# Values loaded once: norms taken from the blocks' own tiles, five staging buffers, a new order

## The chip, the core and the metric

The kernel runs on one core of a Trainium2 chip. A core has TensorE (PE, matmuls), VectorE (DVE), ScalarE (ACT) and GpSimd (POOL), each with an instruction queue of its own that is worked off in order, and SyncE (SP), whose queue issues all the transfers of this kernel. 16 DMA engines move the bytes. The metric is the device time of one execution in microseconds, as the median of several runs.

## The reference

Three stages follow each other: windowed attention with a distance bias, and two feed-forward networks.

```python
# q, k, v: (4, 8, 576, 64)
scores = scale * (q @ k.T)                       # per batch and head, scale = 1/8
mask = (rel >= 0) & (rel < 128)                  # rel = query position - key position
attn = softmax(where(mask, scores + bias, -1e9))
x = (attn @ v) -> (2304, 512)                    # heads side by side

h = x @ w_in                                     # 512 -> 1024
solu = h * softmax(h)
ln = (solu - mean) / sqrt(var + 1e-6) * g_ln
x = ln @ w_out                                   # 1024 -> 512

h = x @ w2_in                                    # 512 -> 2048
out = (h * sigmoid(h)) @ w2_out                  # 2048 -> 512, (2304, 512) float32
```

## The kernel before

The 2304 tokens are 18 blocks of 128 rows; a batch is 4.5 blocks, so that blocks 4 and 13 belong to two batches each. Two blocks make a chunk of 256 tokens for the second network.

Every matmul operand is split into a high and a low float16 part, and three products (high by high, high by low, low by high) stand for one float32 product. For the split a matrix is scaled by a power of two, and that scale comes from a bound on its norm. So each weight has this life. `load_weight` brings it in pieces of 128 x 512 values of 8 bytes (512 KB each) into a staging tile `stage`; `decode` makes float32 of a piece (ACT L456, DVE L458 and L460) in the tile `W`; `gram` (PE L396) multiplies the piece by itself into an accumulator `gram` in PSUM, of which there are two in turn; `trace` or `column_max` (DVE L407, L401) take the bound from it, `norm_scale` the scale; then `split_weight` makes the two parts (L347 to L355, L533). There are 8 pieces of w_in, 8 of w_out, 16 of w2_in and 16 of w2_out, in this order. The staging tiles come from two pools: `early`, and `early2`, which serves some pieces of the first 32 slots only and gives its place to the tiles `g` of the second network later.

The values v go the same way twice. `v_norm(b)` loads batch b in five pieces into tiles `t` (L601) and takes their norm, on PE by `gram` for batches 0 and 1, on ACT by squares (L607) for 2 and 3; `V_AT` says with which block it is ranked. `v_load(i)` loads block i again into a tile `vraw` (L627), of which there are three, and `v_split(i)` makes the two parts `vs` (L347 or L348, and L635).

A block then runs: scores on PE (L681), bias and maximum on DVE (L707), exp on ACT (L712), the softmax's two halves `a` (L342, L343, L354, L355), their transposes by DMA (L739, `aT`), the product with the values (L766), its scaling on DVE (L779), the transpose `xT`, w_in (L813), the layer norm (L827 to L863), its halves and transposes `lnT`. A chunk runs w_out (L913) into `y` (L918, L921), w2_in (L950) with its gate (L959 to L963) and w2_out (L977). A block is joint (`JOINT` is J) if two head pairs' scores share the score tile and L766 writes into `mm1`, the one PSUM buffer that L813 and the layer norm use as well.

No order is written out by hand. `Sched` collects all operations with their dependencies and a rank, which `at` works out from three tables (`RANK`, `SLOPE`, `LATER`), and lists them for each engine in a fixed order before the kernel runs. Strings such as `PICK`, `E_W` and `NORM` say which engine takes an operation that several could. Since each queue is worked off in order, an operation that waits holds everything behind it on its engine; and SP, which issues all loads and transposes, waits in the same manner for a buffer to come free.

```python
more = slot0 < 32 and (at + z) % 3 == 2
st = Buf(early2 if more else early, [P, 512, 2], U32, "stage", N_MORE if more else N_STAGE)
```

Of the kernel before, what the change touches and what calls it, by code (L numbers as in the profile page):

```python
# [17 lines left out]
P = 128  # L18
# [280 lines left out]
def fused_kernel(ctx, tc, qk, qn, kn, vt, rel, w_in, w_out, g_ln, w2_in, w2_out, out):  # L299
# [99 lines left out]
    def column_max(c, acc, f):  # L399
        junk = Buf(early, [P, 4, P], BF16, "junk4", 1)  # L400
        v(552, lambda: V.tensor_tensor_reduce(junk.tile, c.tile.rearrange("p (a b) -> p a b", a=4),  # L401
                                              unit.tile.unsqueeze(1).to_broadcast([P, 4, P]), 1.0, 0.0, ALU.mult, ALU.max,
                                              acc[:, f:f + 1]), [c, unit], [junk, (acc, f)])

    def trace(c, acc):
        junk = Buf(early, [P, P], BF16, "junk", 1)
        v(P + 40, lambda: V.tensor_tensor_reduce(junk.tile, c[:, 0:P], unit.tile, 1.0, 0.0, ALU.mult, ALU.add, acc.tile),  # L407
          [c, unit], [junk, acc])
# [64 lines left out]
    def load_weight(name, w, slot0, n, cols, gain=None, columns=False):  # L473
# [114 lines left out]
    def v_norm(b):  # L588
        s.at("vnorm", V_AT[b])
        on_pe = V_NORM[b] == "P"  # L590
        acc = Buf(const, [P, 1 if on_pe else 5], F32, f"vacc{b}")
        flat = vt[b * S:(b + 1) * S, :].rearrange("a (e f) -> (a e) f", f=256)
        flat = flat.rearrange("(p r) f -> p (r f)", p=P)
        c = Buf(ps_early, [P, 512], F32, "gram", 2) if on_pe else None
        for j, (a, n) in enumerate(((0, 512), (512, 512), (1024, 512), (1536, 512), (2048, 256))):
            def go(j=j, a=a, n=n):
                st = Buf(const, [P, 512], F32, "t", N_T)

                def src():
# [24 lines left out]
    def v_load(i):  # L624
        s.at("vload", i)
# [393 lines left out]
    def block(i):  # L1019
# [6 lines left out]
        v_load(i)  # L1026
# [15 lines left out]
    for c in range(NB // 2 + 1):  # L1042
# [7 lines left out]
        while n < until:  # L1050
# [12 lines left out]
RANK = {"aturn": 8423.8, "av": 1271.8, "evac": -1036.7, "exp": 5647.5, "gate": -1017.5, "in": -427.9, "in2": 228.9,  # L1063
        "load": -3059.8, "lparts": -74.7, "max": -199.5, "max1": 533.1, "norm": -6342.9, "out": -1828.4,
        "out2": 6637.3, "parts": -1334.6, "qk": 3187.5, "s0": 424.5, "s16": 305.7, "s32": 487.6, "s8": 3951.4,
        "share": -1197.1, "store": 1239.0, "table": -3844.1, "tav": -1446.6, "tevac": -831.8, "texp": -470.1,
        "tpar": 2081.3, "tscore": -124.6, "tsub": 2069.8, "vload": 134.1, "vnorm": -2996.0, "vsplit": 736.3,
        "w0": 4797.4, "w16": 195.0, "w32": 887.5, "w8": -8.4, "xturn": -457.7, "y": -155.2}
SLOPE = {"aturn": 52.72, "av": -35.24, "evac": 8.76, "exp": 31.4, "gate": -17.8, "in": 25.51, "in2": -9.86,
         "load": 45.12, "lparts": 17.82, "max": -37.75, "max1": 22.31, "norm": -12.53, "out": 11.91, "out2": 31.11,  # L1070
         "parts": 0.14, "qk": 15.72, "s0": -0.41, "s16": 2.12, "s32": -6.31, "s8": 33.71, "share": 8.67,
         "store": -32.52, "table": 14.94, "tav": 5.28, "tevac": -13.95, "texp": 21.39, "tpar": 19.28, "tscore": 13.35,
         "tsub": -0.49, "vload": 11.22, "vnorm": 13.38, "vsplit": 45.75, "w0": -23.31, "w16": 3.84, "w32": 2.47,
         "w8": 5.05, "xturn": 53.68, "y": -13.59}
# [154 lines left out]
```

## Time and profile before

| | us |
|---|---|
| median of three runs (738.52 to 741.9) | 738.8 |
| the profiled execution | 741.13 |
| its span, from the first to the last instruction | 739.4 |
| PE busy in the span | 681.5 (92%) |
| DVE busy | 446.9 (60%) |
| ACT busy | 350.0 (47%) |
| POOL busy | 134.3 (18%) |

The three runs lie within 0.5% of each other. Busy times are shares of one whole execution, in which the first 150 us look quite different from the rest: weights are brought in, decoded and split there, while the first blocks of attention run between. How much each engine is busy has to be read stage by stage. The granted clock is 1.00 where PE runs at its higher level of 2.4 GHz, and 0.50 at 1.2 GHz; a number between is a mean over the stage.

### The profile page before, as it was taken

The numbers are of one execution on the slowest core, as the hardware profiler recorded it, in microseconds if no ns is written. First come the engines' busy times: TensorE is split into PE (matmuls) and PEld (weight loads), VectorE is DVE, ScalarE is ACT, GpSimd is POOL, SyncE is SP. The second block draws the span as 40 slices with busy tenths as digits, with TensorE's granted clock in tenths as the row PEclk, the third lists the DMA queues.
The fourth block names the chain that finished last, engine by engine and source line by source line (L and its number), as shares of the span: only waits on it lengthen the run. The fifth ranks groups of instructions, "written<-read, shape, count | busy, mean of one in ns | idle before, by whom it ended". The sixth has DMA issues, their size and how long they took to land.

```text
span 739.4 us, 14042 instructions
## 1 busy us (share of the span) xinstructions
PE 681.5 (92%) x5541; PEld 467.1 (63%) x5541; DVE 446.9 (60%) x1141; ACT 350.0 (47%) x742; POOL 134.3 (18%) x131
## 2 busy tenths in 40 slices
PE   3556678899999999999999999999999999999997
PEld 2423347578766586667757765677567666777853
DVE  4689989899799665223655558827556663322230
ACT  5486658685564554244344446517444442232231
POOL 0053215522232401000023102302110210100000
PEclk9997589899999999999999999999999999999999
DMA  9999885357734435041435354527323430200000
GB/s 324 341 296 284 230 258 101 72 146 198 144 58 102 129 70 89 1 146 40 87 79 95 57 116 115 129 43 130 57 59 58 72 74 0 58 16 15 1 29 28
DMA packets 144034, 80.29 MB, mean 109 GB/s; under 512 B 125920, under 2 KB 126560, under 8 KB 143968
## 3 DMA queue, kind: packets, MB, share of 16 engines
q1 hardware_dynamic: 143968, 79.39, 44.5%
q8 instruction: 43, 0.70, 0.4%
q14 instruction: 23, 0.19, 0.1%
HBM read 44.24 MB, written 4.72 MB: 66 GB/s over the span
## 4 chain that ended last, share of the span: by engine, by line
PE 83%; DVE 6%; DMA 5%; ACT 2%; issue 2%; POOL 1%; SPq 1%; DVEq 0%; POOLq 0%; ACTq 0%
PE mm L977 25%; PE mm L950 24%; PE mm L913 13%; PE mm L813 13%; PE sa L681 5%; DMA aT<-a 2%; DMA stage<-in_moe_w_in_dram 2%; PE mm L766 1%; DVE W L460 1%; PE sa L766 1%; DVE e L707 1%; DVE stage L458 1%; DMA t<-in_vt_dram 1%; DMA xT<-x 1%; PE gram L396 1%
## 5 line engine op out<-in xcount | busy, mean ns | idle before, releaser
L950 PE MATMUL mm<-y,W 128*128 128x256 f16 x1728 | 208.0, 273 | 0.1
L977 PE MATMUL mm<-W,g 128*128 128x512 f16 x864 | 204.0, 379 | 0.0
L950 PEld LDWEIGHTS <-W 128*128 128x128 f16 x1728 | 166.2, 98 | 36.3 <-issue 1.0
L977 PEld LDWEIGHTS <-g 128*128 128x128 f16 x864 | 82.2, 98 | 80.0 <-issue 0.5
L913 PE MATMUL mm<-lnT,W 128*128 128x256 f16 x864 | 106.9, 275 | 2.6 <-ACT lnT L568 1.5
L813 PE MATMUL mm<-W,xT 128*128 128x512 f16 x432 | 105.7, 396 | 2.6 <-DMA xT<-x 1.0
L913 PEld LDWEIGHTS <-W 128*128 128x128 f16 x864 | 84.3, 99 | 21.2 <-issue 1.8
L712 ACT ACTIVATE e<-e,mx 128x256 f32<-128x256 f32 (+1 forms) x144 | 70.0, 487 | 52.1 <-DVE mx L707 51.9
L963 DVE SCALAR_TENSOR_TENSOR g<-t,g 128x512 f16<-128x512 f32 x72 | 57.3, 798 | 54.2 <-ACT g L962 53.7
L962 ACT ACTIVATE g<-t 128x512 f16<-128x512 f32 x72 | 45.1, 627 | 91.9 <-PE mm L977 82.6
L355 POOL TENSOR_TENSOR a<-e,a 128x512 f16<-128x512 f32 (+1 forms) x37 | 47.9, 1296 | 183.6 <-DVE a L343 132.5
L960 DVE SCALAR_TENSOR_TENSOR t<-t,mm 128x512 f32<-128x512 f32 x72 | 48.5, 683 | 49.4 <-ACT t L959 49.4
L813 PEld LDWEIGHTS <-xT 128*128 128x128 f16 x432 | 43.3, 102 | 53.5 <-issue 10.5
L959 ACT ACTIVATE t<-mm,cs 128x512 f32<-128x512 f32 x72 | 48.1, 681 | 59.6 <-PE mm L950 59.3
L681 PE MATMUL sa<-k,q 64*128 64x128 f32 x544 | 52.6, 323 | 15.1 <-DVE mx L707 8.1
L707 DVE CUSTOM_DVE_ANT_0 e<-sa,table 128x256 f32<-128x256 f32 (+1 forms) x144 | 53.7, 402 | 18.3 <-PE sa L681 9.4
L681 PEld LDWEIGHTS sa<-k,q 64*128 64x128 f32 x544 | 40.5, 210 | 28.7 <-issue 14.0
L827 DVE TENSOR_REDUCE lnst<-mm 128x1 f32<-128x1024 f32 x18 | 21.9, 1216 | 40.4 <-PE mm L813 40.4
L766 PEld LDWEIGHTS <-aT 128*128 128x128 f16 x816 | 33.1, 101 | 16.1 <-issue 7.9
L921 DVE SCALAR_TENSOR_TENSOR y<-mm,cs,y 128x512 f16<-128x512 f32 x18 | 13.2, 747 | 44.6 <-ACT y L918 44.4
L829 ACT ACTIVATE e<-mm,lnst,sig 128x1024 f32<-128x1024 f32 x18 | 21.6, 1200 | 38.4 <-DVE lnst L828 34.3
L918 ACT ACTIVATE y<-mm,cs 128x512 f16<-128x512 f32 x18 | 12.2, 686 | 55.2 <-PE mm L913 46.6
(149 smaller groups left out, 694.9 us busy)
## 6 DMA issues: line engine op xcount, KB each, us to landing
stage<-in_moe_w_in_dram SPq DMA_DIRECT2D x24, 512.0 KB, 6.6
stage<-in_moe_w_out_dram SPq DMA_DIRECT2D x24, 512.0 KB, 5.3
k<-in_kn_dram SPq DMA_DIRECT2D x18, 256.0 KB, 2.9
q<-in_qn_dram SPq DMA_DIRECT2D x18, 256.0 KB, 3.2
vraw<-in_vt_dram SPq DMA_DIRECT2D x18, 256.0 KB, 3.9
out_dram<-t SPq DMA_DIRECT2D x18, 256.0 KB, 2.0
t<-in_vt_dram SPq DMA_DIRECT2D x16, 256.0 KB, 4.5
aT<-a SPq DMA_TRANSPOSE x72, 3.3
```

Of the source, the lines that this page charges most:

```text
L355: ("G", cg(n), lambda: G.tensor_tensor(dst(), a(), b(), op), True)], r, w, pick=pick)
L681: T.matmul(SA[:, j, off + sl * P:off + (sl + 1) * P], q[rows, p, :], k[rows, p, :], start=True, stop=sl not in blank)
L707: v(n + 20, lambda j=j: V.tensor_tensor_reduce(e[:, j, lo:lo + n], SA[:, j, off + lo:off + lo + n], table[:, 2 * p + j, o:o + n], -0.125, ...
L712: act(n, lambda j=j: A.activation(e[:, j, lo:lo + n], e[:, j, lo:lo + n], AF.Exp, bias=mx[:, j:j + 1], scale=-1.0, accum_out=rs[:, 2 * p + ...
L766: T.matmul(heads(i)[:, h // 4, h % 4, :], t[:, (2 * ha + j) * nh + c, :], vb[sl][:, h, hv, :], start=(n == 0), stop=(n == 3 * nh - 1))
L813: T.matmul(pt[:, half * 512:(half + 1) * 512], x[:, hx, k, :], W16(2 * k + half, hw), start=(k == 0 and hx + hw == 0), stop=(k == KD - 1 a ...
L913: T.matmul(pt[:, ct % 2], W16(8 + k, hw)[:, ct * P:(ct + 1) * P], l[:, hx * KF1 + k, :], start=(k == 0 and hw + hx == 0), stop=(k == KF1 - ...
L950: T.matmul(pt[:, mm], W16(16 + 4 * k + m // 4, hw)[:, (m % 4) * P:(m % 4 + 1) * P], y[:, hx, k, :], start=(k == 0 and hw + hx == 0), stop= ...
L959: act(512, lambda: A.activation(t.tile, flat(pt.tile), AF.Tanh, scale=cs[:, 0:1]), [pt, (cs, 0)], [t], extra=1)
L960: v(512, lambda: V.scalar_tensor_tensor(out=t.tile, in0=t.tile, scalar=1.0, in1=flat(pt.tile), op0=ALU.add, op1=ALU.mult), [t, pt], [t])
L963: v(512, lambda: V.scalar_tensor_tensor(out=flat(g[:, 1]), in0=t.tile, scalar=2.0 ** -16, in1=flat(g[:, 0]), op0=ALU.mult, op1=ALU.subtrac ...
L977: T.matmul(pt.tile, g[:, hg, mm, b * P:(b + 1) * P], W16(32 + m, hw), start=(m == 0 and hg + hw == 0), stop=(m == KF2 - 1 and hg == 1))
```

## The change

`v_norm(b)` no longer loads anything of its own. It calls `v_load` for the blocks of its batch, and takes the norm from their tiles `vraw`, in PE by four gram matmuls per block (only a block's own 64 rows where it is shared), or on ACT by a square of 512 columns per block. The tiles stay until `v_split` has read them, so there are six `vraw` tiles (`N_VRAW`) in place of three. `v_load` returns at once for a block that is there already. The scratch tiles `junk` and `junk4` go; their writers use `sq`. Staging has three buffers and two (`N_STAGE`, `N_MORE`) in place of four and two; two of five pieces go to `early2`, in place of one of three. `V_AT` ranks the norms of batches 1, 2 and 3 with blocks 1, 9 and 10, in place of 0, 7 and 6. The three tables of ranks are new throughout, and so are some entries of the strings that pick engines; blocks 7 and 12 become joint.

```diff
     def column_max(c, acc, f):
-        junk = Buf(early, [P, 4, P], BF16, "junk4", 1)
+        junk = Buf(early, [P, 512], BF16, "sq", 2)
...
-                more = slot0 < 32 and (at + z) % 3 == 2
+                more = slot0 < 32 and (at + z) % 5 in (1, 3)
...
     def v_norm(b):
+        first, stop = b * S, (b + 1) * S
+        here = range(first // P, (stop + P - 1) // P)
+        for i in here:
+            v_load(i)
         s.at("vnorm", V_AT[b])
...
-        flat = vt[b * S:(b + 1) * S, :].rearrange("a (e f) -> (a e) f", f=256)
-        flat = flat.rearrange("(p r) f -> p (r f)", p=P)
-        c = Buf(ps_early, [P, 512], F32, "gram", 2) if on_pe else None
-        for j, (a, n) in enumerate(((0, 512), (512, 512), (1024, 512), (1536, 512), (2048, 256))):
-            def go(j=j, a=a, n=n):
-                st = Buf(const, [P, 512], F32, "t", N_T)
...
-                load(n // 2, lambda: SP.dma_start(src(), flat[:, a:a + n]), [], [st])
+        if on_pe:
+            c = Buf(ps_early, [P, 512], F32, "gram", 2)
+        else:
+            s.op([("G", 150, lambda: G.memset(acc.tile, 0.0), False)], [], [acc])
+        for n, i in enumerate(here):
+            rows = slice(max(0, first - i * P), min(P, stop - i * P))
+
+            def go(n=n, i=i, rows=rows):
+                r = vraw[i]
                 if on_pe:
                     def high(x):
...
-                    gram(c, n // P, high, [st], a // P, 17)
+                        w = r.tile.rearrange("p h d -> p (h d)").bitcast(BF16).rearrange("p (c h) -> p c h", h=2)
+                        return w[rows, x * P:(x + 1) * P, 1]
+                    gram(c, 4, high, [r], 4 * n, 4 * len(here) - 1)
                     return
-                act(n, lambda: A.activation(src(), src(), AF.Square, accum_out=acc[:, j:j + 1]),
-                    [st], [st, (acc, j)], extra=1)
+                junk = Buf(early, [P, 512], BF16, "sq", 2)
+                act(512, lambda: A.activation(junk[rows], r.tile.rearrange("p h d -> p (h d)")[rows], AF.Square,
+                                              accum_out=acc[rows, n:n + 1]), [r], [junk, (acc, n)], extra=1)
...
     def v_load(i):
+        if i in vraw:
+            return
...
-        v_load(i)
         v_split(i)
...
-RANK = {"aturn": 8423.8, "av": 1271.8, "evac": -1036.7, "exp": 5647.5, "gate": -1017.5, "in": -427.9, "in2": 228.9,
+RANK = {"aturn": 8190.5, "av": 1566.9, "evac": -3109.3, "exp": 5884.2, "gate": -1711.8, "in": -283.0, "in2": 763.1,
...
-E_W = "GGGVGGVGGVVGVVGGVGGVVGGVGVGGGGGVVVVGGGGVGGVGGGGG"
+E_W = "GGGGGGVGGVVGVVGGVGGVVGGVGVGGGGGVGVVGGGGVGVVGGGGG"
...
-JOINT = "........JJJJSJJJJJ"
+JOINT = ".......JJJJJJJJJJJ"
...
-N_STAGE = 4
+N_STAGE = 3
...
-N_VRAW = 3
+N_VRAW = 6
...
-V_AT = [0, 0, 7, 6]
+V_AT = [0, 1, 9, 10]
```

The lines of the changed kernel carry numbers some seven higher than those of the kernel before: L634 is the load of `vraw`, L642 its split, L746 the transpose `aT`.

In SP's queue at the program's start, behind the first q and k, there stands in the kernel before (`t` and `vraw` are values, `stage` a piece of a weight, `aT` a transpose of a softmax):

```order
L601 DMA t<-in_vt_dram 128x512 x4
L601 DMA t<-in_vt_dram 128x256
L601 DMA t<-in_vt_dram 128x512
L1002 DMA gcol<-in_moe_g_ln_dram 128x8x1
L627 DMA vraw<-in_vt_dram 128x512 x3
L486 DMA stage<-in_moe_w_in_dram 128x1024 x3
L601 DMA t<-in_vt_dram 128x512
L486 DMA stage<-in_moe_w_in_dram 128x1024
L601 DMA t<-in_vt_dram 128x512
L486 DMA stage<-in_moe_w_in_dram 128x1024
L601 DMA t<-in_vt_dram 128x512
L486 DMA stage<-in_moe_w_in_dram 128x1024
```

It goes on with the last `t`, two transposes and a q between, two `vraw` and the seventh and eighth `stage`. In the changed kernel the same place reads:

```order
L1009 DMA gcol<-in_moe_g_ln_dram 128x8x1
L634 DMA vraw<-in_vt_dram 128x512 x6
L486 DMA stage<-in_moe_w_in_dram 128x1024 x5
L746 DMA_TRANSPOSE aT<-a_137 128x4x128
L746 DMA_TRANSPOSE aT<-a_138 128x4x128
L652 DMA q<-in_qn_dram 128x512
L486 DMA stage<-in_moe_w_in_dram 128x1024
L634 DMA vraw<-in_vt_dram 128x512 x2
L486 DMA stage<-in_moe_w_in_dram 128x1024 x2
```

The ten `t` are gone, eight `vraw` stand where there were five, and the transposes stand ahead of the sixth piece in place of behind it.

In DVE's queue the trace of batch 1's values (`vacc_150`) stands, in the kernel before, between the first two rows of w_out's decoding and the scale of w_in:

```order
L458 TENSOR_SCALAR stage<-stage 128x512
L433 TENSOR_SCALAR nrmb<-mm 128x1
L434 TENSOR_SCALAR nrmc<-nrmb 128x1
L460 SCALAR_TENSOR_TENSOR W<-stage 128x512
L407 ISA junk,vacc_150<-gram,unit 128x128
L407 ISA vacc_150 128x1
L436 TENSOR_SCALAR nrmd<-nrmc 128x1
L438 TENSOR_SCALAR Qwin<-nrmc 128x1
```

In the changed kernel it (`vacc_123`) stands behind the layer norm of block 1, between the two rows (L458, L460) that decode the last piece of w2_in:

```order
L841 SCALAR_TENSOR_TENSOR e_857,lnst<-e_857,lnst,mm_810 128x1024
L458 TENSOR_SCALAR stage<-stage 128x512
L844 TENSOR_SCALAR lnst<-lnst 128x1
L407 ISA sq,vacc_123<-gram,unit 128x128
L407 ISA vacc_123 128x1
L460 SCALAR_TENSOR_TENSOR W<-stage 128x512
L430 TENSOR_REDUCE nrmt<-vacc_123 128x1
```

It moved behind 20 more pieces of weights. Its last tile, block 8's, is issued in the changed kernel's SP queue here, behind the transposes of block 0's layer norm and the last two pieces of w2_in (moe2_w_in, which the rows name like w_in):

```order
L746 DMA_TRANSPOSE aT<-a_794 128x8x128
L888 DMA_TRANSPOSE lnT<-ln_124 128x8x128
L486 DMA stage<-in_moe_w_in_dram 128x1024
L888 DMA_TRANSPOSE lnT<-ln_124 128x8x128
L486 DMA stage<-in_moe_w_in_dram 128x1024
L634 DMA vraw<-in_vt_dram 128x512
L486 DMA stage<-in_moe_w_out_dram 128x1024
```

In the kernel before, all of batch 1 was loaded among the first six pieces.

## Rows read from the trace of the kernel before

**Rows 1.** The page: PE's and the other engines' busy time, share, instructions.

```profile
PE 681.5 (92%) x5541; PEld 467.1 (63%) x5541; DVE 446.9 (60%) x1141; ACT 350.0 (47%) x742; POOL 134.3 (18%) x131
```

**Rows 2.** Table by stage: length, busy us (and instructions) by engine, clock, DMA share, GB/s.

```profile
0.00:18.00 18.00, 7.07 (x47) 5.07 (x47) 8.28 (x39) 10.35 (x28) 1.69 (x12) 1.00 0.92 322
18.00:37.00 19.00, 10.66 (x84) 7.50 (x83) 13.37 (x44) 8.17 (x18) 0.67 (x1) 1.00 1.13 341
37.00:92.00 55.00, 32.85 (x234) 19.06 (x232) 50.23 (x132) 40.88 (x87) 21.91 (x17) 0.78 1.00 270
92.00:143.50 51.50, 42.48 (x355) 28.90 (x354) 46.87 (x116) 36.35 (x73) 20.90 (x20) 0.83 0.58 146
143.50:208.00 64.50, 63.21 (x667) 50.80 (x665) 57.16 (x140) 39.23 (x80) 18.35 (x18) 1.00 0.64 150
208.00:700.00 492.00, 489.65 (x3974) 336.64 (x3971) 263.50 (x662) 205.45 (x443) 70.81 (x65) 1.00 0.34 71
700.00:740.00 40.00, 35.62 (x198) 19.09 (x195) 7.51 (x11) 9.57 (x15) 0.00 (x0) 1.00 0.07 27
```

**Rows 3.** Pieces of the chain that ended last: start us, us, what.

```profile
136.67 6.98 PE mm L813 x24
143.65 1.31 PE mm L950 x12
144.96 0.70 PE sa L766 x24
...
161.63 5.18 PE mm L813 x24
...
243.51 1.09 PE sa L681 x16
```

**Rows 4.** SP's timeline at the start: start us, us of issuing, what.

```profile
8.95 1.48 SPq L486 DMA_DIRECT2D stage<-in_moe_w_in_dram  x3
...
20.91 1.00 SPq L627 DMA_DIRECT2D vraw<-in_vt_dram  x2
22.18 1.60 SPq L486 DMA_DIRECT2D stage<-in_moe_w_in_dram  x2
```

**Rows 5.** DMA issues by tile: count, KB each, median us from issue to landing.

```profile
stage<-in_moe_w_in_dram SPq DMA_DIRECT2D x24, 512.0 KB, 6.6
...
t<-in_vt_dram SPq DMA_DIRECT2D x16, 256.0 KB, 4.5
...
t<-in_vt_dram SPq DMA_DIRECT2D x4, 128.0 KB, 3.8
```

**Rows 6.** ACT's timeline, first step of decoding: start, us, what, idle before, releaser.

```profile
14.62 0.67 ACT L456 ACTIVATE stage<-stage 128x512 f32<-128x512 f32 x1 [0.60 <-DMA stage<-in_moe_w_in_dram]
...
23.41 0.70 ACT L456 ACTIVATE stage<-stage 128x512 f32<-128x512 f32 x1 [1.28 <-DMA stage<-in_moe_w_in_dram]
...
30.17 1.20 ACT L456 ACTIVATE stage<-stage 128x512 f32<-128x512 f32 x2
...
89.08 1.23 ACT L456 ACTIVATE stage<-stage 128x512 f32<-128x512 f32 x2
```

**Rows 7.** Groups by line and form, 0 to 160 us: busy us, mean ns, idle before.

```profile
L707 DVE CUSTOM_DVE_ANT_0 e<-sa,table 128x256 f32<-128x256 f32 x38 | 15.0, 417 | 6.6 <-POOL a L355 2.3 <-PE sa L681 1.6 <-PE sa L687 1.3
...
L533 DVE SCALAR_TENSOR_TENSOR W<-W,sw2in 128x512 f16<-128x512 f32 x6 | 5.1, 876 | 0.0
...
L396 PE MATMUL gram<-t 128*128 128x128 bf16 x36 | 4.6, 307 | 0.0
...
L354 DVE TENSOR_TENSOR W<-W 128x512 f16<-128x512 f32 x6 | 4.1, 683 | 0.0
...
L348 DVE TENSOR_SCALAR W<-W,swin 128x512 f32<-128x512 f32 x4 | 1.9, 477 | 0.0
```

**Rows 8.** All loads into vraw: time from issue to landing.

```profile
DMA to landing us min/median/max: 2.5/3.9/7.0
```

**Rows 9.** SP's waits for a staging buffer: us in total, times, longest us.

```profile
SPq L486 <- DVE W L460: 14.1, 7, 5.2
```

More of the change, by code (lines that the diff above doesn't have):

```diff
@@ L399, in column_max @@
     def column_max(c, acc, f):
-        junk = Buf(early, [P, 4, P], BF16, "junk4", 1)
-        v(552, lambda: V.tensor_tensor_reduce(junk.tile, c.tile.rearrange("p (a b) -> p a b", a=4),
+        junk = Buf(early, [P, 512], BF16, "sq", 2)
+        v(552, lambda: V.tensor_tensor_reduce(junk.tile.rearrange("p (a b) -> p a b", a=4), c.tile.rearrange("p (a b) -> p a b", a=4),
                                               unit.tile.unsqueeze(1).to_broadcast([P, 4, P]), 1.0, 0.0, ALU.mult, ALU.max,
@@ L405, in trace @@
     def trace(c, acc):
-        junk = Buf(early, [P, P], BF16, "junk", 1)
-        v(P + 40, lambda: V.tensor_tensor_reduce(junk.tile, c[:, 0:P], unit.tile, 1.0, 0.0, ALU.mult, ALU.add, acc.tile),
+        junk = Buf(early, [P, 512], BF16, "sq", 2)
+        v(P + 40, lambda: V.tensor_tensor_reduce(junk[:, 0:P], c[:, 0:P], unit.tile, 1.0, 0.0, ALU.mult, ALU.add, acc.tile),
           [c, unit], [junk, acc])
@@ L1062 @@
 PITCH = 3.3
-RANK = {"aturn": 8423.8, "av": 1271.8, "evac": -1036.7, "exp": 5647.5, "gate": -1017.5, "in": -427.9, "in2": 228.9,
[L1064 to L1074, printed above, removed]
@@ new lines @@
+RANK = {"aturn": 8190.5, "av": 1566.9, "evac": -3109.3, "exp": 5884.2, "gate": -1711.8, "in": -283.0, "in2": 763.1,
+        "load": -4397.6, "lparts": -1653.6, "max": 176.2, "max1": 339.6, "norm": -7961.4, "out": -1027.6,
+        "out2": 3298.4, "parts": -1379.1, "qk": 1402.7, "s0": -168.5, "s16": 369.8, "s32": 455.6, "s8": 3931.6,
+        "share": -1605.8, "store": 2439.7, "table": -5196.2, "tav": 59.2, "tevac": -749.8, "texp": 4157.2,
+        "tpar": 3201.3, "tscore": -1216.6, "tsub": 333.9, "vload": 753.3, "vnorm": -2520.6, "vsplit": 128.2,
+        "w0": 1479.2, "w16": 76.9, "w32": 998.7, "w8": -63.2, "xturn": -869.5, "y": -1911.0}
@@ new lines @@
+SLOPE = {"aturn": 47.79, "av": -25.89, "evac": -5.68, "exp": 11.77, "gate": -21.88, "in": 36.34, "in2": -11.62,
+         "load": 10.3, "lparts": 18.87, "max": -24.94, "max1": -2.34, "norm": -4.0, "out": 15.06, "out2": 30.48,
+         "parts": -23.26, "qk": 32.18, "s0": 3.76, "s16": 1.95, "s32": 6.94, "s8": 26.54, "share": 17.85,
+         "store": -34.37, "table": 17.51, "tav": -5.62, "tevac": 7.06, "texp": 19.15, "tpar": 25.04, "tscore": 5.66,
+         "tsub": 13.31, "vload": 7.87, "vnorm": 15.99, "vsplit": 25.91, "w0": -6.05, "w16": 1.69, "w32": -8.51,
+         "w8": -8.24, "xturn": 39.68, "y": -12.6}
```

103 lines of the change are left out of this document (49 added, 54 removed), and 43 rows, old and new, of the table LATER.

## The prediction

> **What bounds the kernel now.** I read the page's busy line first, then the table by stage, then the chain of waits, and only then single lines. TensorE (PE) is busy 681.5 us of a span of 739.4 [rows 1], so at most some 58 us can be won without taking PE work away. The stages tell where they lie [rows 2]. From 143.5 us on PE stands still for 1.3 us up to 208, for 2.4 us in the 492 us after that, and for 4.4 us at the end. Ahead of 143.5 it stands still for 10.9 + 8.3 + 22.2 + 9.0 = 50.4 us. There the granted clock is 0.78 and 0.83 too, as a mean of the two levels: a group of 24 L813 matmuls takes 6.98 us at 136.67 where it takes 5.18 at 161.63 [rows 3]. So the start is what can be won, and the mark to watch is the first L950, at 143.65 [rows 3]: from there on there is nearly always PE work to do.
>
> What holds the start? The DMA engines are full (a share of 0.92, 1.13 and 1.00) up to 92 us, and the most they move is 341 GB/s [rows 2]. VectorE (DVE) is busy only 8.3 of 18 and 13.4 of 19 us in the first 37 us, but 50.2 of 55 and 46.9 of 51.5 after them. So it is the transfers up to about 37 us, and DVE, at 91%, from there to the mark. ScalarE has 74% and 71% there, which leaves it room.
>
> **The change part by part.** *A, values loaded once.* Twenty transfers into t (16 of 256 KB, 4 of 128 KB) go [rows 5], and the 18 into vraw, one per block, stay. The t pieces of two batches stand at the start. Ahead of the eighth piece of the first weight there stand, by the order, 9156 KB before (2304 of them t, and five vraw) and 7620 now (no t, eight vraw): 1536 KB or 1.57 MB less. At 0.322 to 0.341 MB per us [rows 2] this is 4.6 to 4.9 us. It counts where decoding waits for landings. ScalarE did so for each of the six pieces from 14.62 to 23.41 [rows 6], the first of them issued at 8.95; the next two ran only at 30.17, because they were issued at 22.18, behind two transposes and two vraw [rows 4, 6]. DVE has 15.4 idle us in this stretch. Not all of the 4.7 arrives, since the same SP queue still has two transposes and two vraw ahead of the eighth piece. I take -3.5, bounds -4.9 and 0.
>
> The rate is worth a second look, in sentences that the sum does without. The best stage of the trace has 341 GB/s [rows 2]. The Trainium skill, "DMA: Bandwidth & Descriptors", Specifications, gives about 358 GB/s from HBM as one core's share; by that the saving would be an estimated 4.4 us in place of 4.7, and the term -3.3 in place of -3.5.
>
> What A adds has cover. Four more gram matmuls (40 for 36, since block 4 counts for two batches) are 4 x 0.31 us [rows 7] on an engine that idles there: 0, without that cover 1.2. The squares of batches 2 and 3 on ScalarE (ten of 512 columns for eight and two halves) move to blocks 9 and 10, where ScalarE is busy 205 of 492 us: 0, without cover less than 1. Two memsets on POOL at the program's start: 0. SP has 20 issues fewer, which only empties its queue.
>
> *B, the order.* I counted each engine's rows up to the same marks in both orders and priced them with this trace. PE: ahead of the end of the fourth L813 group the new order has 8 fewer score matmuls (-1.09), 12 more L766 (+0.35) and 12 L950 (+1.31) [rows 3]; that is +0.6 us, the same within what a row is worth. So PE has as much behind that mark as before, and the gain is how much sooner it comes. DVE, up to the second row of y (L921), which all L950 wait for: 4 fewer scalings of weights (-1.9), 2 fewer fused subtractions (-1.8), 2 fewer score rows with their read-outs (-1.0), a decode row less (-0.5) and a few softmax halves (-1.1), against 2 more casts and 2 more subtractions of at most 0.68 each (+2.5) and small rows (+1.4): -2.4 us [rows 7]. At two later marks, the fifth and the eleventh L960, DVE leads by 5 and 17 us, but PE then has 7 and 13 us more left, so nothing is added for them. ScalarE has about 2 us more ahead of the same y, out of its 30% of idle time. I take -2, bounds 0 and -4 (some 2 of the 9.0 us in which PE waits from 92 to 143.5 go as well, since 12 L950 now run ahead of the fourth L813 group).
>
> *C, what the buffers cost.* The six vraw tiles push one staging buffer out: five in place of six while the first 32 pieces come, and three in place of four for the last 16, since the second pool serves slots below 32 alone. A piece takes 6.6 us to land [rows 5] and about 2 to be decoded, so five buffers bring one in 1.7 us. Before, pieces 7 to 32 came from 30.17 to 89.08 [rows 6], one in 2.4 us, so the loss there is 0. In the first 37 us, where 512 KB are 1.6 us of transfer, it is 0.1 a piece, up to 1 for the first eight. SP waits 14.1 us in the whole program for DVE to give such a buffer back, at most 5.2 at a time [rows 9], and what stands behind on SP waits too: the transposes aT that L766 needs. Bounds 0 and +4; I take +0.5.
>
> *D, a new wait.* The norm of batch 1 needs block 8. Its tile is issued behind the last w2_in piece, into a buffer that block 2's split gives back, and its trace (L407) now stands in DVE's row between two decode rows; three of the four column maxima of w2_in wait behind it, since the gram buffers take turns. Between block 2's split and this trace DVE has about 12 us of rows, and a vraw lands in 2.5 to 7.0 us [rows 8]. So I take 0, bounds 0 and +10 (the first rival).
>
> *E, the middle.* Blocks 7 and 12 become joint: L766 then writes into mm1, the one buffer that L813 and the layer norm use. PE loses 2.4 us from 208 to 700 now [rows 2]; I take 0, bounds -1 and +2.
>
> Sum: -3.5 - 2 + 0.5 = -5.0 us on the span of 739.4, which gives 734.4. The profiled run took 741.1 in all, 1.7 around its span; the median of the runs is 738.8, and the same -5.0 puts it at **733.8**.
>
> **The rivals.** *Block 8 late (slower).* SP is in order: if it stands at a staging buffer (up to 5.2 us in one wait), has two lnT transposes ahead, and the tile then lands in 7.0 us, DVE reaches L407 first and stands, with decoding, softmax and w2_in's scale behind it, on the engine that sets the start. It decides from 8.7 us of lateness (the 5.0 won, and the 3.7 that are 0.5%). At 10 us: 738.8 - 5 + 10 = 743.8. For it speaks that this load is behind the last of 16; against it the 12 us of DVE rows, and that PE and DVE have other rows until there.
>
> *Hidden anyway (no change).* From 37 us on DVE is 91% busy whatever comes sooner. If pieces that land sooner only wait for DVE, A brings nothing and B's -2 remains: 738.8 - 2 = 736.8. For it: SP already waits for DVE's decoding [rows 9], so landings were not always what came last. Against it: DVE's 15 idle us ahead of 37.
>
> *More than that.* A and B at their best, -4.9 and -4, and nothing given back: 729.9. It needs PE to go on without a hole from the first L950.
>
> **How the numbers follow.** 0.5% (3.7 us) is about what a measurement of this kernel can tell from no change. Around my forecast (-3.7 to -7.5 us): 0.38. The best case: 0.14. Hidden: 0.31. Late, or another stall of that size: 0.17. So faster 0.52, same 0.31, slower 0.17. The range runs from 729.0 to 742.5, which leaves out some 0.03 below and the 0.17 above; the likeliest case's own range is 731.3 to 735.1.
>
> **What would show it.** A: the eighth piece decoded by 27 us in place of 30.2, DVE's idle time in the first 37 us down from 15.4 to about 12. B: the first L950 between 126 and 137 us in place of 143.65, with PE busy from there. C: SP's waits for decode rows no longer than before. D: no idle DVE time over 2 us ahead of batch 1's L407. E: PE idle for less than 4 us from 208 to 700. The forecast is wrong if the first L950 comes no sooner than 140, if DVE stands ahead of that trace, or if PE loses in the middle what the start has won.

## The result, and the profile after

The changed kernel takes **731.6 us** (median of four runs, 729.4 to 733.0) where the kernel before takes 738.8 (now of four runs): a ratio of 0.989, 95% interval 0.9854 to 0.9927. That is 7.2 us less; forecast were 5.0 less and 733.8, with a range of 729.0 to 742.5. The profiled execution after took 729.4 us in all, 2.2 below its median, and that of before 2.3 above its own, so the two traces lie 11.9 us of span apart (727.5 and 739.4), 4.7 more than the medians. A second profiled execution of the changed kernel, in experiment 1, lies at the median (731.8, span 729.9); its number is given beside where the two differ. The runs of the kernel before lie in two clusters, around 739.3 us at a mean granted clock of 0.976 to 0.979 and around 742.8 at 0.960 to 0.972, and its median falls into the one or the other by the group of runs, so that the gap to the changed kernel is 7 to 10 us.

The page's busy line after, to hold against [rows 1]:

```profile
PE 674.3 (93%) x5541; PEld 464.0 (64%) x5541; DVE 444.8 (61%) x1125; ACT 346.2 (48%) x738; POOL 138.5 (19%) x140
```

The table by stage after, to hold against [rows 2] (length, busy us and instructions of PE, PEld, DVE, ACT, POOL, granted clock, DMA share, GB/s):

```profile
0.00:18.00 18.00, 7.54 (x49) 5.39 (x49) 6.35 (x35) 10.37 (x30) 2.42 (x15) 1.00 0.95 310
18.00:37.00 19.00, 10.70 (x87) 7.73 (x88) 16.48 (x44) 11.84 (x27) 4.45 (x5) 1.00 1.06 341
37.00:92.00 55.00, 32.35 (x232) 18.08 (x231) 53.09 (x132) 41.47 (x90) 11.91 (x13) 0.80 0.97 253
92.00:143.50 51.50, 45.96 (x452) 35.11 (x451) 50.75 (x125) 34.51 (x67) 20.30 (x19) 0.95 0.64 159
143.50:208.00 64.50, 62.60 (x620) 47.69 (x618) 56.49 (x139) 42.68 (x95) 22.27 (x22) 1.00 0.59 132
208.00:700.00 492.00, 491.44 (x3990) 338.27 (x3988) 256.90 (x648) 199.00 (x424) 77.20 (x70) 1.00 0.33 65
700.00:740.00 40.00, 23.70 (x122) 11.73 (x120) 4.74 (x7) 6.31 (x10) 0.00 (x0) 0.99 0.07 27
```

DVE's idle time tells most. In the first 37 us it fell only from 15.4 to 14.2 us (15.1 in experiment 1), but from 37 to 92 from 4.8 to 1.9, and from 92 to 143.5 from 4.6 to 0.75. The marks of [rows 3] in PE's timeline after (L957 is L950 of before, L820 is L813):

```profile
124.62 1.26 PE L957 MATMUL mm<-y,W 128*128 128x256 f16 x6 [0.18 <-DVE y L928]
...
128.16 5.39 PE L820 MATMUL mm<-W,xT 128*128 128x512 f16 x24
```

The first L957 stands at 124.6 (143.65 before). The fourth group of 24, behind which PE has the same work in both kernels, ends at 128.16 + 5.39 = 133.6, and at 136.67 + 6.98 = 143.65 before [rows 3]: 10.1 us sooner, 9.0 in the second execution. From there to the end both need about the same: 593.9 us after (595.2 in experiment 1), 595.7 before. So it is the start that got shorter, as forecast.

To see where, here is the stretch from 37 us to the end of the second row of y (L921, L928), which all L950 wait for. Before:

```profile
37.00:131.87 94.87, 65.27 (x543) 42.74 (x540) 85.98 (x229) 69.91 (x142) 35.32 (x32) 0.82 0.86 228
```

After:

```profile
37.00:124.57 87.57, 59.90 (x526) 40.00 (x526) 85.33 (x226) 65.60 (x137) 24.64 (x26) 0.86 0.86 223
```

y is there 7.3 us sooner; the other 2.8 of the 10.1 us lie between y and that mark, and they belong to the granted clock (see *The clock* below). DVE was busy 86.0 of 94.9 us before and is busy 85.3 of 87.6 now: its holes shrank from 8.9 to 2.2 us, its work by hardly anything (with the first 37 us, 107.6 and 108.2 us). The holes of before, in DVE's timeline (idle time and what ended it in brackets), were mostly waits for PE and POOL; the four longest of them:

```profile
53.27 0.42 DVE L707 CUSTOM_DVE_ANT_0 e<-sa,table 128x256 f32<-128x256 f32 x1 [1.05 <-POOL a L355]
70.19 0.69 DVE L779 TENSOR_TENSOR xm<-sa,rinv 128x512 f32<-128x512 f32 x1 [1.45 <-PE sa L681]
92.67 1.23 DVE L827 TENSOR_REDUCE lnst<-mm 128x1 f32<-128x1024 f32 x1 [1.05 <-PE mm L813]
109.14 1.22 DVE L827 TENSOR_REDUCE lnst<-mm 128x1 f32<-128x1024 f32 x1 [1.66 <-PE mm L813]
```

The longest that is left after:

```profile
71.23 0.42 DVE L714 CUSTOM_DVE_ANT_0 e<-sa,table 128x256 f32<-128x256 f32 x1 [0.89 <-PE sa L773]
```

### The profile page after: what moved, and what is told of

Read it like the earlier page. It is cut to its first block, busy times and chain, and to the rows that moved or that the text cites. A ratio compares the mean times of both kernels' runs of the same rounds, so it can differ in the third digit from the quotient of the medians.

```text
span 727.5 us, 13956 instructions
## 1 busy us (share of the span) xinstructions
PE 674.3 (93%) x5541; PEld 464.0 (64%) x5541; DVE 444.8 (61%) x1125; ACT 346.2 (48%) x738; POOL 138.5 (19%) x140
## 4 chain that ended last, share of the span: by engine, by line
PE 79%; DVE 14%; ACT 3%; issue 2%; DMA 1%; POOL 0%; DVEq 0%; POOLq 0%; ACTq 0%
PE mm L984 25%; PE mm L957 23%; PE mm L920 12%; PE mm L820 11%; PE sa L688 4%; DVE W L460 3%; PE mm L773 2%; DVE stage L458 2%; DVE e L714 1%; PE gram L396 1%; DVE W L533 1%; PE sa L773 1%; DVE W L354 1%; DMA aT<-a 1%; DVE W L348 1%
## 5 line engine op out<-in xcount | busy, mean ns | idle before, releaser
L957 PE MATMUL mm<-y,W 128*128 128x256 f16 x1728 | 210.4, 273 | 1.1 <-DVE t L967 0.7
L984 PE MATMUL mm<-W,g 128*128 128x512 f16 x864 | 204.9, 379 | 0.0
L957 PEld LDWEIGHTS <-W 128*128 128x128 f16 x1728 | 167.0, 98 | 39.8 <-issue 2.0
L984 PEld LDWEIGHTS <-g 128*128 128x128 f16 x864 | 81.8, 98 | 78.7 <-issue 0.2
L820 PE MATMUL mm<-W,xT 128*128 128x512 f16 x432 | 105.2, 390 | 1.7 <-DVE xT L569 1.0
L920 PE MATMUL mm<-lnT,W 128*128 128x256 f16 x864 | 104.8, 273 | 0.0
L970 DVE SCALAR_TENSOR_TENSOR g<-t,g 128x512 f16<-128x512 f32 x72 | 55.5, 774 | 53.7 <-ACT g L969 53.3
L355 POOL TENSOR_TENSOR a<-e,a 128x512 f16<-128x512 f32 (+1 forms) x45 | 54.9, 1222 | 143.2 <-ACT a L342 65.8
L820 PEld LDWEIGHTS <-xT 128*128 128x128 f16 x432 | 42.7, 100 | 47.6 <-issue 4.6
L688 PE MATMUL sa<-k,q 64*128 64x128 f32 x544 | 49.4, 312 | 17.1 <-DVE mx L714 12.2
L714 DVE CUSTOM_DVE_ANT_0 e<-sa,table 128x256 f32<-128x256 f32 (+1 forms) x144 | 53.9, 400 | 11.3 <-PE sa L688 6.3
L688 PEld LDWEIGHTS sa<-k,q 64*128 64x128 f32 x544 | 38.5, 202 | 29.1 <-DVE mx L714 15.7
L928 DVE SCALAR_TENSOR_TENSOR y<-mm,cs,y 128x512 f16<-128x512 f32 x18 | 13.3, 748 | 57.1 <-ACT y L925 57.1
L834 DVE TENSOR_REDUCE lnst<-mm 128x1 f32<-128x1024 f32 x18 | 22.0, 1220 | 42.0 <-PE mm L820 42.0
L848 POOL TENSOR_SCALAR lnst<-lnst 128x1 f32<-128x1 f32 x17 | 3.5, 203 | 214.0 <-ACT mm L845 214.0
```

What stands on the lines that cost most here:

```text
L355: ("G", cg(n), lambda: G.tensor_tensor(dst(), a(), b(), op), True)], r, w, pick=pick)
L688: T.matmul(SA[:, j, off + sl * P:off + (sl + 1) * P], q[rows, p, :], k[rows, p, :], start=True, stop=sl not in blank)
L714: v(n + 20, lambda j=j: V.tensor_tensor_reduce(e[:, j, lo:lo + n], SA[:, j, off + lo:off + lo + n], table[:, 2 * p + j, o:o + n], -0.125, ...
L820: T.matmul(pt[:, half * 512:(half + 1) * 512], x[:, hx, k, :], W16(2 * k + half, hw), start=(k == 0 and hx + hw == 0), stop=(k == KD - 1 a ...
L920: T.matmul(pt[:, ct % 2], W16(8 + k, hw)[:, ct * P:(ct + 1) * P], l[:, hx * KF1 + k, :], start=(k == 0 and hw + hx == 0), stop=(k == KF1 - ...
L957: T.matmul(pt[:, mm], W16(16 + 4 * k + m // 4, hw)[:, (m % 4) * P:(m % 4 + 1) * P], y[:, hx, k, :], start=(k == 0 and hw + hx == 0), stop= ...
```

## The experiments

Twelve kernels, in groups that ran on one chip beside runs of the kernel before: 1 to 4, 5 to 8, 9 to 11, and 12. A ratio is to the kernel before of the same group. Unless it is said otherwise, every engine's row keeps its place in the changed kernel's order (in experiment 3, in that of the kernel before). In experiments 5 to 7 and 12 the order is listed first as the changed kernel has it, and the edit shown takes effect behind that; the lines that do so are left out here. Line numbers of the experiments are some 4 to 20 higher than those of the changed kernel.

**1. The changed kernel again.** No edit.

> The changed kernel once more, as the measure for the others of this call. Both theories (the bytes count; the order counts) expect what was measured first: 731.6 us, 0.989 of the kernel before, and a profile in which the fourth group of 24 L820 ends near 133.6 us (143.7 before).

Measured: 731.75 us (730.2 to 733.3), 0.9863 (0.9838 to 0.9888). The number stands. The kernel before had 742.1 in this group (739.0 to 743.8), so the gap is 10.3 us here. Its stretch to the second y:

```profile
37.00:125.88 88.88, 59.81 (x526) 39.99 (x526) 86.41 (x226) 66.69 (x138) 25.58 (x26) 0.86 0.87 224
```

**2. The bytes put back.**

```diff
+DEAD = {('v', 1): 1, ('v', 3): 1, ('v', 5): 1, ('w', 1): 1, ('w', 2): 1, ('w', 3): 1}
...
+            for _ in range(DEAD.get((kind, n), 0)):
+                z = issued["dead"] = issued.get("dead", 0) + 1
+                SP.dma_start(W[:, NSLOT + LAG - z, :], vt[z * P:(z + 1) * P, :])
```

> The changed kernel with six loads of 256 KB of values put back into its start (1.57 MB, into rows of W that are written again much later, read by nobody); every other instruction in the changed kernel's order. The bytes count: those 4.7 us of transfer come back in part, the time is 3 to 5 us above the changed kernel's (735 to 737). The order counts and the bytes were hidden: at most 1 us above it (732 to 733), since DVE, 98% busy from 37 us to the second row of y in the changed kernel's trace, is the limit there.

Measured: 734.1 us (732.1 to 735.4), 0.9893 (0.9868 to 0.9918): 2.4 above experiment 1 (some 1 to 3.5 by the scatter of the runs), between the two expectations and with overlapping ranges. The trace agrees with the size: y comes at 128.1, 2.2 later than in experiment 1.

```profile
37.00:128.08 91.08, 61.50 (x527) 41.00 (x526) 87.59 (x228) 67.61 (x140) 25.89 (x27) 0.83 0.88 231
```

DVE's holes from 37 us to y are 91.08 - 87.59 = 3.5 us here, against 2.5 in experiment 1 and 8.9 before: they stay small with the bytes back. This kernel is also the change without the saving, that is the order with the new buffers and joint blocks: it is still 8.0 us (interval 6.1 to 9.8) faster than the kernel before of its group, of 10.3 for the whole change. A load put back brings its transfer and also its issue on SP (0.33 to 0.61 us each in this trace); how the 2.4 us divide between the two is not shown, here or in experiment 3.

**3. Fewer bytes in the kernel before.**

```diff
+                if b == 1:
+                    s.op([("SP", 420 if n > 256 else 600, lambda: G.memset(src(), 1.0), False)], [], [st],
+                         dma=max(n // 2 * 3.5, 364))
+                else:
+                    load(n // 2, lambda: SP.dma_start(src(), flat[:, a:a + n]), [], [st])
```

> The kernel before without the five loads of batch 1's values at its start (1.15 MB less); POOL writes ones into these tiles instead, so batch 1's scale comes from ones and not from its values. The order of all other instructions is that of the kernel before. The bytes count: 1.15/1.57 of the term A of -3.5, so -2.6 us (736 where the kernel before takes 738.8). The bytes were hidden: within 1 us of the kernel before.

Measured: 740.0 us (736.5 to 741.8), 0.9969 (0.9949 to 0.9989): 2.1 less than before (0.8 to 3.8 by the interval), for 1152 KB, which are 1.18 MB and not the 1.15 of the expectation. So these loads do count, in either order: some 2 to 3 us for 1.57 MB, not the 3.5 that I took. With the order of before DVE's holes stayed: 93.44 - 85.05 = 8.4 us from 37 us to y, which came at 130.4, 1.4 us sooner than before.

```profile
37.00:130.44 93.44, 64.44 (x530) 42.69 (x529) 85.05 (x225) 69.14 (x141) 35.32 (x32) 0.82 0.88 220
```

**4. More work for DVE.**

```diff
+            if pick[0] == "wl" and twice["wl"] <= TWICE:
+                V.tensor_tensor(dst(), a(), b(), op)
```

> The changed kernel with six subtractions on DVE (L354, W<-W, 0.68 us each, 40 to 87 us) done twice in a row: 4.1 us of DVE work more, the result is the same. If DVE's row of work now sets the start (idle for 2.2 us in all from 37 us to the second y): +3.5 to +4.1 us (735 to 736). If transfers or PE set it: at most +1.

Measured: 736.7 us (735.8 to 737.7), 0.9928 (0.9901 to 0.9954): 5.0 above experiment 1, for 4.1 us of DVE. What is added to DVE ahead of y is paid in full.

**5 and 6. Six and four staging buffers** in place of five.

```diff
-                more = slot0 < 32 and (at + z) % 5 in (1, 3)
+                more = slot0 < 32 and (at + z) % 2 == 1
...
-N_MORE = 2
+N_MORE = 3
-N_T = 6
+N_T = 5
```

> The changed kernel with six staging buffers for the first 32 pieces (N_MORE 3, every second piece into the second pool) in place of five, every engine's order that of the changed kernel; to make room, five t buffers in place of six. If five buffers hold the start back: 1 to 3 us less than the changed kernel (729 to 731), with the sixth piece issued before the 16.7 us at which it now waits for the first one's decoding. If not, within 1 us of it. The step C of the prediction (+0.5) lies between.

Measured: 731.7 us (731.0 to 733.9), 0.9893 (0.987 to 0.9915). No gain, though SP issued the sixth piece 1.5 us sooner than in experiment 1 (at 16.2 and 17.7 us). Its profiled execution was the slowest of its six (733.9); y came at 128.3 there, 2.5 later than in experiment 1, so that it is the median and not the trace that says that the sixth buffer is worth nothing. The t buffer that it lacks costs nothing either: behind the fourth L813 group its trace has 595.4 us, and that of experiment 1 has 595.2.

```diff
-                more = slot0 < 32 and (at + z) % 5 in (1, 3)
+                more = slot0 < 32 and (at + z) % 4 == 1
...
-N_MORE = 2
+N_MORE = 1
```

> The same with four staging buffers (N_MORE 1, every fourth piece into the second pool), order unchanged. If landings from about 37 us on are hidden behind DVE: up to 2 us more than the changed kernel (732 to 734). If a buffer's turn is what limits the pieces (6.6 us of landing and 2 of decoding over four buffers are one piece in 2.2 us, about the pace of DVE): 4 us more or above.

Measured: 738.8 us (737.1 to 740.0), 0.9979 (0.9962 to 0.9996): some 7 us more. DVE's holes from 37 us to y are 96.55 - 88.30 = 8.3 us:

```profile
37.00:133.55 96.55, 62.44 (x527) 41.12 (x527) 88.30 (x230) 68.78 (x141) 27.14 (x27) 0.82 0.81 221
```

So there is an edge between five and four: the step that the change made (six to five) was free, the next would have cost nearly the whole gain.

**7. Three subtractions from DVE to POOL.**

```diff
-        "wl": "VVVGVVGVGGG...
+        "wl": "VGVGVGGGGGG...
```

> The changed kernel with three subtractions of w_in's rows (L354, 0.68 us each on DVE, 41 to 45 us) done by POOL (L355, 1.15 us each), POOL being busy 11.9 of 55 us there; the order is otherwise the same. DVE sets the start: 1.5 to 2 us less (730). If the first L820 group waits for POOL's rows, and DVE for its L834: no gain, or a loss of up to 2.

Measured: 733.6 us (732.1 to 734.6), 0.9912 (0.989 to 0.9934): no gain, rather 1 to 2 us lost. DVE's work up to y stayed what it was (108.9 us, 108.3 in experiment 1), although 2.0 us of rows were gone: the rows that ran beside POOL's took 12.8 us longer than is usual for their kind, for 10.8 in experiment 1. Experiment 12 has the counterpart. Its idle time up to y grew by 2.5 us, of which waits for PE are the main part.

**8. Block 8's tile late.** The dead loads of experiment 2, eight of them, just ahead of its load.

```diff
+DEAD = {('w', 32): 8}
```

> The changed kernel with eight loads of 256 KB (into rows of W that are written again later) just ahead of block 8's tile on SP: its tile lands some 6 to 10 us later (2.1 MB at 0.25 to 0.34 MB per us, 0.4 us of issuing each). In the changed kernel's trace it landed 1.3 us ahead of its first gram. The rival 'block 8 late' as priced in the prediction: DVE stands at L407 and the time is 5 to 9 us above the changed kernel (737 to 741). If other rows cover it: at most +2.

Measured: 735.6 us (734.9 to 737.4), 0.9934 (0.9911 to 0.9957): 3.9 above experiment 1. DVE's timeline has the wait:

```profile
94.73 0.29 DVE L415 CUSTOM_DVE_ANT_0 sq<-gram,unit 128x128 bf16<-128x128 f32 x1 [3.20 <-PE gram L404]
```

In experiment 1 the tile was issued at 82.5 and landed 6.7 us later, 1.3 us ahead of its gram at 90.5. Here it was issued at 88.8 and landed after 5.3: 4.9 us later. 4.9 - 1.3 = 3.6 us of lateness, 3.2 of waiting at L407, 3.9 in the time; another 0.8 us is a wait for a piece that the eight loads held up behind it. The changed kernel does not wait here, but 1.3 us is all that it has.

**9. PE kept busy in its holes.**

```diff
+WARM = {(2, 0): 14, (2, 1): 4, (2, 2): 18, (2, 3): 4, (3, 1): 6, (3, 3): 5, (4, 1): 6}
...
+                for _ in range(WARM[i, p]):
+                    T.matmul(idle, ones.tile, table.tile.rearrange("p a b -> p (a b)")[:, 0:512], start=True, stop=True)
```

> The changed kernel with 57 matmuls of 512 columns behind seven groups of L688, where PE stands still (57 to 75, 86, 100 and 122 us); they write into a buffer mm that nobody reads, the order of all else is unchanged. In the profile of the changed kernel the granted clock is at the lower level from 60.0 to 80.5, 90.7 to 94.1 and 124.8 to 128.3 us, each time behind a hole in PE's work; the second L820 group (77.7 to 84.0) and the matmuls ahead of it run there. If the clock falls with PE's holes and costs time on the path: these stretches go or shrink, and the time is 1.5 to 3 us below the changed kernel (728 to 730). If DVE covers PE's slower work: within 1 us of it, whatever the clock. If the added matmuls stand in the way: up to 2 more.

Measured: 733.4 us (732.5 to 734.0), 0.9894 (0.9865 to 0.9923): not faster, but 1.6 above experiment 1. The clock did what was meant. In the changed kernel (granted clock is the number behind POOL's):

```profile
60.00:80.50 20.50, 9.42 (x49) 5.42 (x50) 19.30 (x48) 17.62 (x40) 6.21 (x7) 0.50 0.94 232
```

With PE kept busy:

```profile
60.00:77.50 17.50, 11.62 (x78) 5.57 (x75) 16.69 (x39) 15.67 (x34) 7.18 (x8) 1.00 0.92 243
...
142.30:145.80 3.50, 3.50 (x19) 2.52 (x17) 3.50 (x8) 1.43 (x3) 0.00 (x0) 0.51 0.57 178
```

The lower level is gone from 60 to 77.5 us, and yet y came at 125.57 in place of 125.88: ahead of y PE's slow stretch was hidden behind DVE. A new short fall stands at 142.3, behind y and behind a hole of 2.4 us in PE's work: 48 L957 matmuls took 7.07 us there, for 5.40 in experiment 1. Behind the fourth L813 group the trace has 597.9 us in all, for 595.2, and so more is lost there than the 0.6 us by which this group came sooner.

**10. Blocks 7 and 12 not joint.**

```diff
-JOINT = ".......JJJJJJJJJJJ"
+JOINT = "........JJJJSJJJJJ"
```

> The changed kernel with blocks 7 and 12 computed as in the kernel before (not joint), its order kept up to block 7's scores and as near as the buffers let it behind them. The step E of the prediction (0, -1 to +2 for the change) expects the changed kernel's time within 1 us. If the joint blocks took PE's holes out of the middle (2.4 us from 208 to 700 before, 0.6 to 1.8 after): 1 to 2 us more.

Measured: 741.0 us (739.7 to 742.2), 1.0 (0.9982 to 1.0018): 9.2 above experiment 1, which neither side expected. Up to the first L984 it is the same kernel (193.1 us, 192.5 in experiment 1). Most of the loss lies at the end. Here, and then after:

```profile
600.00:738.50 138.50, 128.58 (x907) 88.12 (x905) 35.05 (x62) 35.78 (x55) 2.87 (x3) 1.00 0.07 20
```

```profile
600.00:727.50 127.50, 123.69 (x844) 82.22 (x842) 32.03 (x57) 32.05 (x50) 2.86 (x3) 1.00 0.08 21
```

PE stands still for 9.9 us there in place of 3.8, and in the whole run it is busy 677.6 us in place of 674.1. The waits of that stretch (PE waiting for whom, us in total, times, longest) name DVE's gate rows:

```profile
PE mm L961 <- DVE t L971: 5.0, 7, 1.2
```

Without the joint blocks the order behind block 7 came out another, so this run tells that the order of the end is worth 6 us and more, not what the joint blocks are worth. That stays open.

**11. The old ranks.** RANK, SLOPE and LATER of the kernel before in the changed one.

```diff
-RANK = {"aturn": 8190.5, ...
+RANK = {"aturn": 8423.8, ...
```

> The changed kernel with the three tables of ranks of the kernel before: values loaded once and five staging buffers, but not the new order. If the bytes were the main part: at most 3 us above the changed kernel (735). If the order is (some 5 us of the gain by the marks of the traces, and what the old ranks do with buffers they were not made for): 5 us above it or more (737 and up), with DVE idle for 5 us or more from 37 us to the second y.

Measured: 763.9 us (761.5 to 766.0), 1.0307 (1.027 to 1.0345): 32 us more, y at 154.5, with DVE idle for 11.9 us from 37 us to y. The old order doesn't fit the new loads and buffers, so this is no price of the new order alone; it shows that with the old ranks the new loads bring no gain.

**12. Six subtractions from POOL to DVE,** two scalings from POOL to ScalarE: the counterpart of experiment 7.

```diff
-        "al": "VGVGGGGGGGGVGGVG...
+        "al": "VGVGVVVGGVGVGGVV...
...
-        "xl": "GGGG...
+        "xl": "VGGG...
```

In "wc", the entries 17 and 30 turn from G to A.

> The changed kernel with six of POOL's subtractions (L355, five of softmax rows and one of x, 34 to 106 us) done by DVE (L354, 0.68 us each: +4.1 us of DVE rows) and two of POOL's scalings (107.7 and 108.6 us) by ScalarE, every order kept. In the changed kernel's trace the DVE rows that ran beside these took 0.8 to 0.96 us longer each, until POOL's row was over (5.4 us beside the six, 0.8 beside the two). If that lengthening is POOL's doing: -5.4 - 0.8 + 4.1 = some -2 us up to the second row of y (122.5 to 123.5 where the changed kernel has 124.6 and 125.9) and 1 to 2 us less in all (730). If the rows are long for another reason: +4 us of DVE work, paid as the six doubled rows were: 736.

Measured: 731.6 us (729.9 to 734.0), 0.9877 (0.9855 to 0.9899): the changed kernel's time. The lengthening was POOL's doing, but its end brought nothing. DVE's timeline in experiment 1, then POOL's beside it:

```profile
35.46 1.19 DVE L343 CAST a<-e 128x512 f16<-128x512 f32 x1
...
36.91 2.67 DVE L458 TENSOR_SCALAR stage<-stage 128x512 uint32<-128x512 uint32 x2
```

```profile
35.22 1.15 POOL L355 TENSOR_TENSOR a<-e,a 128x512 f16<-128x512 f32 x1
36.79 1.21 POOL L355 TENSOR_TENSOR a<-e,a 128x512 f16<-128x512 f32 x1 [0.42 <-POOL a L355]
37.97 1.33 POOL L355 TENSOR_TENSOR x<-xm,x 128x512 f16<-128x512 f32 x1
```

The same DVE rows in experiment 12, without POOL beside them:

```profile
35.80 0.42 DVE L361 CAST a<-e 128x512 f16<-128x512 f32 x1
...
37.07 0.42 DVE L476 TENSOR_SCALAR stage<-stage 128x512 uint32<-128x512 uint32 x1
```

1.19 became 0.42, and 2.67 for two became 0.42 each. DVE's work up to y fell by 3.4 us, although six rows were added. Yet y came no sooner (127.1 and 125.9), since the holes grew from 2.5 to 7.3 us:

```profile
37.00:127.08 90.08, 62.42 (x526) 40.97 (x526) 82.76 (x231) 67.58 (x141) 19.58 (x19) 0.76 0.84 221
```

DVE then waited for PE: for L838 (L820 of the changed kernel), the score matmuls and the products with the values, 5.8 us in all. PE's 526 matmuls of that stretch took 62.4 us here, for 59.8 in experiment 1. So DVE alone does not set the start: with some 2 us of holes it was about level with PE's chain, and less work on it moved the wait. How much of the wait is PE's slower pace in this one execution is not shown; the median of six runs shows no gain. Nor did a faster PE alone bring y sooner by more than 0.3 us (experiment 9); both together were not tried. No kernel here beats the changed one.

## Why the prediction was right in sum and wrong in its split

The sum held (-5.0 forecast, -7.2 measured), and the place (the start, up to the first L950) did. Its terms did not: A was about 1 us too large and C 0.5, B 2.8 us or more too small; that these errors cancel as far as they do is luck.

- **What bounds the kernel**: right. Of the 11.9 us between the two traces, 10.1 are won by the end of the fourth L813 group, which ended at 143.65. Two readings of the working were off, without weight for the sum: up to that mark the traces have 16 score matmuls fewer (144 and 128), not 8, and 16 is also what the -1.09 prices; and PE's 4.4 idle us at the end are 3.8, since the span ends at 739.4.
- **A, the values loaded once (-3.5)**: right in kind, too large. Experiment 2 gives 2.4, experiment 3 gives 2.1 for 1.18 MB; both hold the loads' issue on SP too, which I had put at nothing. The eighth piece's first step was to be done by 27; it starts near 27.9 (near 30.7 before), as ACT's timeline after shows against [rows 6]:

```profile
25.20 0.65 ACT L456 ACTIVATE stage<-stage 128x512 f32<-128x512 f32 x1
...
27.31 1.79 ACT L456 ACTIVATE stage<-stage 128x512 f32<-128x512 f32 x3
```

  DVE's idle time ahead of 37 us was to fall to 12 and is 14.2 (15.1 in experiment 1). What I had not seen is a new wait. The norm of batch 0 now needs five whole tiles and their 20 grams, and its trace stands in DVE's row ahead of the first piece's decoding, which had landed at 13.0. DVE's timeline after:

```profile
14.56 0.29 DVE L407 CUSTOM_DVE_ANT_0 sq<-gram,unit 128x128 bf16<-128x128 f32 x1 [2.53 <-PE gram L396]
...
16.03 0.68 DVE L460 SCALAR_TENSOR_TENSOR W<-stage 128x512 uint32<-128x512 uint32 x1
```

  It stood there for 2.5 us; before, the trace was done at 12. SP's sixth piece waited in turn for the buffer that this decoding gives back; what this costs in the time no run shows (SP's timeline after):

```profile
14.88 0.59 SPq L652 DMA_DIRECT2D q<-in_qn_dram  x1
16.74 0.33 SPq L486 DMA_DIRECT2D stage<-in_moe_w_in_dram  x1
```

- **B, the order (-2, bounds 0 and -4)**: the step that failed. The order, with the buffers and joint blocks that came with it, is worth some 5 us or more: 7.2 less A's 2.4 is 4.8, and experiment 2 has it at 8.0 (6.1 to 9.8). The first L950 came at 124.6 (125.9 in experiment 1), sooner than the 126 to 137 that I had named. I had priced the order by DVE's rows up to y, -2.4 us. The rows did fall (303 for 311), by 1.5 us if each counts with the usual duration of its kind in its own trace (1.3 in experiment 1). But rows that ran beside POOL's took 10.8 us more than usual, for 9.1 before, and so DVE's busy time did not fall (+0.5 us). What fell were DVE's holes, from 8.9 to 2.2 us, and I had no term for those: I had read DVE as 91% busy and left the other 9% out, though it was more than the sum. That the holes went with the order (and the buffers that came with it) and not with the bytes, experiments 2 (bytes back, 3.5 us of holes) and 3 (order of before with fewer bytes, 8.4) show; which of the new ranks closed which hole stays open.
- **C, the staging buffers (+0.5)**: 0, by experiment 5; experiment 6 has the edge that the bound +4 was for, one buffer further. The check that I gave for it was wrong. SP's waits for decode rows did grow, from 24.5 us (14.1 in [rows 9], and 10.4 for L458 in the same view) to 36.7, and cost nothing that a sixth buffer would have saved (26.0 in experiment 5, in the same time):

```profile
SPq L486 <- DVE stage L458: 22.5, 13, 5.7
SPq L486 <- DVE W L460: 14.2, 11, 2.8
```

- **D, block 8's tile (0)**: right, and no idle time stands ahead of that trace. But the cover that I named, 12 us of DVE rows, was 1.3 us by the time the tile had landed. *Block 8 late* was a fair rival with a fair price: 3.6 us of lateness cost 3.9.
- **E, the joint blocks (0)**: PE's idle time from 208 to 700 us is 0.6 (1.8 in experiment 1, 2.4 before), inside the bounds. What of it is theirs stays open.
- **The clock** had no term either. In the profiled execution of before PE fell to the lower level once more behind y, from 133.4 to 140.2, where PE is the bound, and the fourth L813 group took 6.98 us for 5.18. Below are that fall, the stretch from y to the end of this group before, and the same 46 matmuls of the same order in experiment 3, where the clock was 1.00:

```profile
133.40:140.20 6.80, 6.12 (x25) 3.32 (x26) 6.29 (x17) 4.07 (x13) 3.27 (x3) 0.50 0.47 116
...
131.87:143.65 11.78, 10.20 (x46) 5.36 (x47) 11.27 (x21) 7.34 (x21) 7.59 (x6) 0.71 0.28 67
```

```profile
130.44:139.28 8.84, 7.27 (x46) 4.04 (x47) 8.84 (x19) 6.41 (x19) 5.28 (x5) 1.00 0.34 89
```

  The changed kernel needs 9.0 us from y to the end of that group (8.8 in experiment 1). So the fall cost some 3 us on the path in that one execution, and the 10.1 us between the marks are 7.3 won and 2.8 of clock. That is part of why the two traces are further apart than the medians.
- *Hidden anyway* fell: bytes put back cost time. *More than that* (729.9) came closest of the rivals, not by A and B at their best but by a smaller A and a B beyond its bounds.

## What to carry to other kernels

Where an engine is 90% busy ahead of the mark that counts, price a new order by that engine's holes too, one by one with what ends each, and not by its rows alone: here the rows gave -2.4 us and DVE's work stayed the same, while its holes shrank by 6.7. Before giving a buffer up, look for the edge by taking one more away: six to five was free, five to four cost 7 us. And when two engines are about level, work added to one can be paid in full (experiment 4) while work taken off it brings nothing (experiment 12).

## What the runs showed of the hardware

DVE rows of 0.42 us took 1.19 to 1.38 us when a POOL subtraction of 1.15 to 1.33 us ran beside them (experiment 1, 35 to 40 us), and ended 0.3 us behind POOL's row. Up to y such lengthening sums to 10.8 us in experiment 1 (14 rows, each over 1.4 times and 0.25 us above the median of its kind in the trace), to 3.5 (5 rows) in experiment 12 and to 9.1 (15 rows) in the kernel before. POOL's rows got longer as well, where DVE's were there first: that subtraction takes 1.15 to 1.16 us in most places, 1.33 to 1.51 in others, and 2.67 in the kernel before, where four DVE rows of such kinds followed each other beside it. This is the row for which DVE then waited at 53.27 (POOL's timeline before):

```profile
50.57 2.67 POOL L355 TENSOR_TENSOR a<-e,a 128x512 f16<-128x512 f32 x1 [4.33 <-ACT a L342]
```

Other DVE rows ran beside POOL's at the length that they have elsewhere: in experiment 1 a reduction of 1.20 us (L834) at 112.83, and a row of L714 of 0.40 at 117.76. The Trainium skill, "SBUF — State Buffer", SBUF: two separate sides, says that DVE instructions in a mode with two ports, or with two inputs in SBUF, share a pair of ports with GpSimd under an exclusive lock that the first to start holds for its whole instruction, while the other is blocked. The traces agree with the blocking, in both directions. The Trainium skill, "Perfetto Trace Analysis", Optimizing Scalar/DVE Operations, warns that moving work between these two might not help. Experiment 7 agrees: three rows of 0.68 us moved to POOL made the time no shorter, and DVE's work up to y, with 2.0 us of rows gone, was 108.9 us for 108.3.

The granted clock in the records does not tell the whole of TensorE's pace at the start. All of the first 60 us read 1.00 after, yet four L396 matmuls take 0.61 us at 16.77 and 0.40 at 56.18. In experiment 12, whose PE rows are the same, the mean clock of the stretch from 18 to 37 us reads 0.51, and PE's 87 matmuls are busy for 10.69 us there, for 10.70 at a clock that reads 1.00 after.
